# Slot order, channel-major share and recompute lead in a two-pass ConvNeXt-V2 block

## The chip, the cores and the metric

The kernel runs on one core of a Trainium2 chip. The metric is the device time of one execution in microseconds, given as the median of five runs. PE is the matrix engine, ACT the engine of activations, DVE the vector engine, POOL the general engine (GpSimd), SP the engine that here only issues DMAs.

## The reference

The input is one image of 512 x 512 pixels with 96 channels in bf16. E is 4 x 96 = 384.

```python
for i in range(K):
    for j in range(K):
        out = out + xp[:, i:i+H, j:j+W, :] * dw[i, j][None, None, None, :]
h = _layernorm(out, axis=-1)
h = jnp.einsum('bhwc,ce->bhwe', h, w1)
h = _gelu(h)
gx = jnp.sqrt((h * h).sum(axis=(1, 2), keepdims=True) + 1e-6)
nx = gx / (gx.mean(axis=-1, keepdims=True) + 1e-6)
h = grn_gamma * (h * nx) + grn_beta + h
h = jnp.einsum('bhwe,ec->bhwc', h, w2)
return x + h
```

A depthwise 3 x 3 convolution, LayerNorm over the channels, an expansion to 384 channels with GELU, a global response normalisation (GRN), a contraction to 96 channels and a residual. GRN needs, for each of the 384 channels, the sum of squares over all pixels of the image, so nothing of the contraction can start before the whole image has been expanded once.

## The kernel before

The image is cut into 128 blocks of four rows (2048 pixels). A block's pixels are handled as four quarters ("quads") of 512 columns. There are two passes.

**First pass.** A loop over slots s (lines 721 to 834); every engine executes its instructions in the order in which the program issues them (`InOrder`, line 22). In the steady state slot s does these things for different blocks:

- It convolves block s on PE in three bursts of 24 small matmuls (`conv_taps`, line 408), which all write one PSUM tile Y; the pool of Y has one buffer. After bursts 0 and 1 PE is drained (`pe.drain`, line 441). ACT copies Y to the SBUF tile `y_bf` (`evac`, line 443). Burst 0 of block s also reads rows of block s+1.
- DVE turns x of block s+2 to channels on partitions (`turn_x`, line 387).
- PE sums y and y squared over the channels for an earlier block (`stage_stats`, line 462, 24 matmuls of 4 columns) into the columns S of the PSUM tile SG; POOL makes the square `ysq`. After each batch of four blocks DVE reads the sums and clears S (`stage_moments`, line 474, a scaling and a memset), POOL works out the reciprocal deviation, DVE turns it (`stage_turn`, line 549), SP spreads it by DMA, and POOL multiplies (`stage_norm`, line 581).
- It expands one normalised block b, about 14 slots behind the convolution (`mlp_units`, line 611). The 2048 x 384 results are made in six expansions, each of two PSUM banks (pool `psU`, two buffers of two banks) and one GELU on ACT: `pair(0..2)` make quarters 0 and 1 with channels on the partitions ("channel-major"), 128 channels at a time, into `gsh`; `rest(0..2)` make the other two quarters into `gm`. A third quarter may be channel-major too (`cm_quads`, line 91): then the first half of `gm` is channel-major and the second half pixel-major. The pixel-major part has pixels on the partitions and 384 columns for each of four groups of 128 pixels in a quarter.
- It adds up squares for GRN in two ways. Channel-major quarters: DVE's bn_stats (`squares`, `squares_rest`), three for each quarter, entries collected 32 at a time and then aggregated by DVE (`combine`, line 671, three bn_aggr). Pixel-major quarters: PE multiplies each 128 x 128 piece by itself into a Gram accumulator whose diagonal is the sum (`gram_mms`, line 664), 12 matmuls a quarter, into the remaining columns of the tile SG. S (128 columns) and the Gram columns (384) fill one PSUM bank together. The Gram work of block b is done in the slot after its own.
- SP stores quarter 0 of `gsh` in HBM (`g_dram`).

The pools of `gsh` and `gm` have three buffers each. Blocks 126 and 127 are kept in SBUF (`is_res`) and are treated apart. From slot 128 on there is no convolution left, and the slots only expand.

**Second pass.** A loop over the blocks (line 898), kept ones first. For each block the contraction runs in four sub-steps of 48 / 4 = 12 matmuls into O (`stage_mm2`, line 282); DVE adds O to `xb` and SP writes the result. POOL loads x again and adds a bias to it (`stage_xb`, line 274). Quarter 0 comes back from HBM; quarters 1 to 3 are expanded again from the stored normalised input: three units a block, each of three matmuls of 512 columns and one GELU of 1536 columns (`recompute_units`, line 254). There are 384 units. After each sub-step `pace` (line 330) issues as many units as its formula asks for; they run ahead of the contraction by a lead that begins at LEAD = 8 units (line 316). `advance` never goes further than five blocks ahead.

The order in a slot that both convolves and expands (lines 782 to 815), as PE sees it: conv(0), pair(0), pair(1), conv(1), pair(2), conv(2), rest(0), statistics, rest(1), Gram of the block before, rest(2). ACT: pair 0, 1, 2, the copy of Y, rest 0, 1, 2.

Of the kernel before, what the change touches and what calls it, by code (L numbers as in the profile page):

```python
# [53 lines left out]
def kernel(  # L54
# [17 lines left out]
    E = w1.shape[1]  # L72
# [5 lines left out]
    NBLK = H // GR  # L78
# [9 lines left out]
    def is_res(q):  # L88
        return q >= NBLK - RES

    def cm_quads(q):
        return 3 if q % 3 and not is_res(q) else 2

    def kept_quads(q):
        return 2 if is_res(q) else 1
# [64 lines left out]
    with ExitStack() as p1:  # L160
# [74 lines left out]
        NSUB = PXP // GPS  # L235
# [82 lines left out]
        total = len(todo)  # L318
# [10 lines left out]

        def pace(n, sub):  # L330
            due = sum(1 for v in todo if v <= n + 1) if sub == NSUB - 1 else 0
            even = LEAD + (n * NSUB + sub + 1) * (total + 2 - LEAD) / (NSUB * NBLK)
            advance(max(due, even), n + PRE)

        SG = psS.tile([128, 2 * NS + NCH * 128], f32, name="SG")
# [72 lines left out]
        def conv_taps(b, spare):  # L408
            if spare:
                Ua = psU.tile([128, 2, W], f32, name="U")  # L410
                Ub = psU.tile([128, 2, W], f32, name="U")
                Y = [Ua[:, 0, :], Ua[:, 1, :], Ub[:, 0, :]]
            else:
                Y3 = psY.tile([128, NI, W], f32, name="Y")
                Y = [Y3[:, i, :] for i in range(NI)]
            mms = []
            for n in range(3):
                mms.append([(h, j, (n + h) % NI, dx) for dx in (0, -1, 1) for j in range(GR) for h in range(2)])
            flat = [m for ms in mms for m in ms]
            first = {}  # L420
            last = {}
            for n, (h, j, i, dx) in enumerate(flat):
                first.setdefault((i, j), n)
                last[i, j] = n

            def burst(n):
                k = sum(len(ms) for ms in mms[:n])
                for h, j, i, dx in mms[n]:
                    src = b + shift(h, j)
                    o0, o1 = max(0, -dx), W - max(0, dx)  # L430
                    pe.matmul(
                        Y[i][32 * j:32 * j + 32, o0:o1],
                        lhsT=Wq[64 * h:64 * h + 64, i, dx + 1, j, :],
                        rhs=x_rows(src, 64 * h, 64 * h + 64, i, MB * (1 + dx) + o0, o1 - o0)
                        if 0 <= src < NBLK else zrow[64 * h:64 * h + 64, o0:o1],
                        start=first[i, j] == k,
                        stop=last[i, j] == k,
                    )
                    k += 1
                if n < 2:  # L440
                    pe.drain()

            def evac():
                y = ypool.tile([128, NI, W], bf16, name="y_bf")
                if spare:
                    act.activation(out=y[:, 0:2, :], in_=Ua[:], func=ACTF.Identity)
                    act.activation(out=y[:, 2, :], in_=Ub[:, 0, :], func=ACTF.Identity)
                else:
                    act.activation(out=y[:], in_=Y3[:], func=ACTF.Identity)
                ybf[b] = y  # L450

            return [lambda n=n: burst(n) for n in range(3)], evac

        def stage_sq(b, on_act):
            q = ysqpool.tile([128, NI, W], bf16, name="ysq")
# [152 lines left out]
        def px0(b):  # L608
            return NCH * QW * (cm_quads(b) - 2)
# [51 lines left out]

            return pair, rest, squares, squares_rest, store

        def gram_mms(b):
            for k in range((TAIL - px0(b)) // E):
                for j in range(NCH):
                    c = px0(b) + k * E + j * 128
                    v = gms[b][:, c:c + 128]
                    pe.matmul(gram[:, j, :], lhsT=v, rhs=v, start=False, stop=True, skip_group_check=True)
# [51 lines left out]
        for s in range(last_slot + 1):  # L721
            get = lambda kind: at.get((s, kind), [])
            if s + 4 < NBLK:
                load_x(s + 4)
            for b in get("read"):
                stage_read(b)
            for b in get("write"):
                stage_write(b)
            for k in get("bcast"):
                stage_bcast(k)  # L730
            for k in get("rows"):
                stage_rows(k)
            if store:
                store()
                store = None
            for k in get("moments"):
                stage_moments(k)
            for k in get("newton"):
                stage_newton(k, pool)
            for b in get("norm"):  # L740
                stage_norm(b)
            for b in get("sqp"):
                stage_sq(b, False)
            for k in get("rstd"):
                stage_rstd(k, pool)
            mlp = get("mlp")

            def spread_out():
                for k in get("spread"):
                    stage_spread(k)  # L750
                for b in get("norma"):
                    stage_norm(b)

            spare = not mlp and s % 2 == 1
            taps, evac = conv_taps(s, spare) if s < NBLK else ([], None)
            if not mlp:
                for f in taps:
                    f()
                if not spare:
                    spread_out()  # L760
                if evac:
                    evac()
                for b in get("sqa"):
                    stage_sq(b, True)
                if s + 2 < NBLK:
                    turn_x(s + 2)
                for b in get("stats"):
                    stage_stats(b)
                if spare:
                    spread_out()  # L770
                for k in get("chain"):
                    stage_moments(k)
                    stage_chain(k)
                for k in get("turn"):
                    stage_turn(k)
                for b in get("gram"):
                    gram_mms(b)
            else:
                b = mlp[0]
                pair, rest, squares, squares_rest, put_out = mlp_units(b)  # L780
                conv = lambda n: taps[n]() if taps else None
                conv(0)
                pair(0)
                pair(1)
                if not taps:
                    for b2 in get("gram"):
                        if b2 != b:
                            gram_mms(b2)
                squares(0)
                conv(1)  # L790
                spread_out()
                if s + 2 < NBLK:
                    turn_x(s + 2)
                pair(2)
                squares(1)
                for k in get("turn"):
                    stage_turn(k)
                conv(2)
                if evac:
                    evac()  # L800
                rest(0)
                squares(2)
                for b2 in get("stats"):
                    stage_stats(b2)
                rest(1)
                if taps:
                    for b2 in get("gram"):
                        if b2 != b:
                            gram_mms(b2)
                rest(2)  # L810
                squares_rest()
                for b2 in get("gram"):
                    if b2 == b:
                        gram_mms(b2)
                if not is_res(b):
                    store = put_out
            if s == 1:
                setup_mlp()
            if s == 4:
                setup_rest()  # L820
            for b in get("combine"):
                combine(b)
            if s == last_slot - 3:
                pc.close()
                late.psO = p2.enter_context(tc.tile_pool(name="psO", side="right", bufs=2, space=bass.MemoryType.PSUM))
                late.xr = p2.enter_context(tc.tile_pool(name="xr", side="right", bufs=5))
                late.xb = p2.enter_context(tc.tile_pool(name="xb", side="right", bufs=3))
                late.gr = p2.enter_context(tc.tile_pool(name="gr", side="right", bufs=4))
                late.gl = p2.enter_context(tc.tile_pool(name="gld", side="right", bufs=6))
                late.o = p2.enter_context(tc.tile_pool(name="o", side="right", bufs=4))  # L830
            for n in {2: (0, 1, 2), 1: (3, 4)}.get(last_slot - s, ()):
                stage_load(n, sp, pool)
            if s == last_slot - 1:
                for n in range(RES):
                    stage_xb(ORDER[n], pool, B2bc_f)
# [104 lines left out]
```

## Time and profile before

| | |
|---|---|
| median of five runs | 1566.23 us (1563.24 to 1571.81) |
| profiled execution, its own time | 1563.24 us |
| profiled execution, span from first to last instruction | 1561.5 us |
| granted PE clock, mean | 0.996 |
| busy: PE, ACT | 1449.5 us, 1447.2 us (93% each) |
| busy: POOL, DVE | 1315.7 us (84%), 1129.5 us (72%) |
| bn_stats on channel-major quarters | 1020 instructions, 468.7 + 156.5 + 7.3 us |
| Gram matmuls | 2064, 136.3 us |
| slots with convolution and expansion | about 104 to 937 us |
| slots with expansion alone | 937 to about 1018 us |
| second pass | about 1020 to 1561 us |

The profile shows one execution on the chip. Times in it are microseconds from the first instruction. "Busy" of an engine is the time in which at least one of its instructions runs; instructions of one engine overlap a little at their ends, so the durations of single instructions add up to more than the time that a run of them takes. A line of a timeline gives the start, the time, the engine, the line of the code (L32 is the helper that issues all ordered instructions), the operation with its tiles, and in brackets how long the engine was idle before and what ended the wait.

### The profile page before, as it was taken

How to read it: one execution, taken by the hardware profiler on the slowest of the kernel's cores; microseconds unless marked ns; L12 is line 12 of the kernel's file. 1: busy time of each engine (PE TensorE's matmuls, PEld its weight loads, DVE VectorE, ACT ScalarE, POOL GpSimd, SP SyncE). 2: the span in 40 equal slices, each digit the busy share in tenths (PEclk: the TensorE clock that was granted, in tenths of full speed). 3: DMA queues.
4: the chain of work that ended last, by engine and by line, in shares of the span. 5: the costliest groups of instructions: out<-in, count | busy, mean ns of one | idle time of the engine just before them, and what ended most of it. 6: DMA issues, size and time to landing. Idle time of an engine off the chain costs nothing. (4 is left out here: it accounts for less than half of the span.)

```text
span 1561.5 us, 55720 instructions
## 1 busy us (share of the span) xinstructions
PE 1449.5 (93%) x23749; PEld 843.8 (54%) x23749; DVE 1129.5 (72%) x2027; ACT 1447.2 (93%) x1306; POOL 1315.7 (84%) x933
## 2 busy tenths in 40 slices
PE   7889999999999999999999997789999999999997
PEld 3444444444444444444444444457777777777765
DVE  6748978888898888889888888855555555555544
ACT  3889989999999999999999999999999999999996
POOL 3559888988989898998889887559999999999994
PEclk8999999999999999999999999999999999999999
DMA  5668787787778788777778667879999999999994
GB/s 147 183 186 262 233 253 221 241 256 213 238 237 250 214 249 253 221 236 239 230 225 249 209 189 221 280 252 391 388 390 391 385 395 385 384 379 390 383 369 147
DMA packets 235470, 427.94 MB, mean 274 GB/s; under 512 B 34102, under 2 KB 148374, under 8 KB 235222
## 3 DMA queue, kind: packets, MB, share of 16 engines
q1 hardware_dynamic: 219972, 356.59, 70.1%
q0 software_dynamic: 13888, 67.64, 11.4%
q8 instruction: 186, 3.05, 0.8%
q14 instruction: 62, 0.51, 0.1%
q10 hardware_dynamic: 1362, 0.15, 0.1%
HBM read 272.78 MB, written 150.72 MB: 271 GB/s over the span
## 5 line engine op out<-in xcount | busy, mean ns | idle before, releaser
L32 PE MATMUL U<-ynT,w1p 128*128 128x512 bf16 x2166 | 601.7, 380 | 44.1 <-ACT gm L32 8.4
L32 DVE BATCH_NORM_STATS2 bst<-gsh 128x6 f32<-128x512 bf16 x756 | 468.7, 673 | 128.3 <-ACT gsh L32 127.7
L32 ACT ACTIVATE gr<-U 128x1536 bf16<-128x1536 f32 (+1 forms) x384 | 521.1, 1450 | 16.3 <-PE U L32 14.2
L32 POOL TENSOR_TENSOR yn<-y_bf,rbc 128x1536 bf16<-128x1536 bf16 x128 | 397.2, 3106 | 83.5 <-ACT rbc L32 30.3
L32 DVE TENSOR_TENSOR o_sb<-O,xb 128x384 bf16<-128x384 f32 x512 | 277.6, 557 | 252.5 <-PE O L32 175.7
L278 POOL TENSOR_TENSOR xb<-xr,B2c 128x1536 f32<-128x1536 bf16 x126 | 395.1, 3137 | 38.0 <-DVE B2c L32 29.9
L32 ACT ACTIVATE gsh<-U 128x1024 bf16<-128x1024 f32 x378 | 369.5, 1024 | 55.3 <-ACT gm L32 29.2
L32 ACT ACTIVATE gm<-U 128x1024 bf16<-128x1024 f32 x384 | 367.9, 1033 | 0.1
L32 PE MATMUL Y<-xT,Wq 64*32 64x511 bf16 (+1 forms) x8694 | 321.4, 389 | 8.5 <-DVE B2bc_f L32 3.7
L32 POOL TENSOR_TENSOR ysq<-y_bf 128x1536 bf16<-128x1536 bf16 x114 | 313.4, 2750 | 13.8 <-ACT y_bf L32 13.5
L32 PEld LDWEIGHTS <-w1p 128*128 128x128 bf16 x2166 | 169.1, 97 | 277.6 <-issue 177.8
L32 PEld LDWEIGHTS <-gr 128*128 128x128 bf16 x4584 | 228.7, 98 | 84.9 <-ACT gr L32 12.1
L32 PE MATMUL O<-W2s,gr 128*128 128x96 bf16 x4584 | 251.4, 206 | 12.4 <-ACT gr L32 9.4
L32 PEld LDWEIGHTS <-Wq 64*32 64x32 bf16 x9216 | 101.9, 90 | 186.5 <-issue 145.8
L32 PE MATMUL U<-w1p,ynT 128*128 128x384 bf16 (+2 forms) x1032 | 161.3, 272 | 33.6 <-ACT gm L32 30.5
L32 ACT ACTIVATE y_bf<-Y 128x1536 bf16<-128x1536 f32 x121 | 175.1, 1447 | 16.6 <-PE Y L32 16.4
L32 DVE STREAM_TRANSPOSE xT<-xin 128x576 f32<-128x576 f32 (+1 forms) x256 | 181.3, 747 | 2.9 <-DMA xin<-in_x_dram 2.8
L32 DVE BATCH_NORM_STATS2 bst<-gm 128x6 f32<-128x512 bf16 x252 | 156.5, 677 | 0.9 <-ACT gm L32 0.9
L32 PEld LDWEIGHTS <-ynT 128*128 128x128 bf16 x1032 | 88.6, 97 | 90.8 <-issue 69.3
L32 PE MATMUL SG<-gm 128*128 128x128 bf16 x2064 | 136.3, 219 | 0.5 <-ACT gm L32 0.3
L32 PEld LDWEIGHTS <-gm 128*128 128x128 bf16 x2064 | 121.0, 98 | 11.5 <-issue 0.5
L250 POOL DMA_DIRECT2D xr<-in_x_dram x123 | 67.9, 552 | 27.6 <-POOL xb L278 27.6
(103 smaller groups left out, 700.7 us busy)
## 6 DMA issues: line engine op xcount, KB each, us to landing
ynT<-yn_dram SPq DMA_DIRECT2D x254, 384.0 KB
xin<-in_x_dram SPq DMA_DIRECT2D x126, 432.0 KB
yn_dram<-yn SPq DMA_DIRECT2D x512, 96.0 KB
xr<-in_x_dram POOLq DMA_DIRECT2D x128, 384.0 KB, 6.6
out_dram<-o_sb SPq DMA_DIRECT2D x127, 384.0 KB
g_dram<-gsh SPq DMA_DIRECT2D x126, 384.0 KB
gl<-g_dram SPq DMA_DIRECT2D x84, 384.0 KB
gl<-g_dram POOLq DMA_DIRECT2D x42, 384.0 KB, 6.7
```

The costliest lines, as they stand in the source:

```text
L32: r = f(*a, **k)
L250: pq.dma_start(out=xr[:], in_=x[0, r0:r0 + GR].rearrange("r w c -> (r w) c").rearrange("(p g) c -> p g c", g=PXP))
L278: pq.tensor_tensor(out=xb[:], in0=grp[q]["xr"][:], in1=bias[:, None, :].to_broadcast([128, PXP, C]), op=ALU.add)
```

## The change

Three things are changed.

1. Every block that is not kept in SBUF now has three channel-major quarters. Before, blocks whose number is divisible by three had two.
2. The order inside a slot that expands is another one. PE's new order is conv(0), pair(0), conv(1), pair(1), first half of the Gram matmuls of the block before, pair(2), second half, rest(0), conv(2), rest(1), statistics, rest(2). ACT's is pair 0, 1, 2, rest(0), the copy of Y, rest(1), rest(2). On DVE the transposes of x come ahead of the squares of pair(0), and the turn of the reciprocal deviation comes after the squares of pair(2). Where there is no convolution, the Gram matmuls stay together ahead of pair(2).
3. In the second pass the pace formula no longer lets the lead shrink from 8 units to 2: it stays at 8 until the units run out.

The bursts of the convolution also take an argument that can leave out the drain; no caller in the program sets it, so the drains stay.

```diff
     def cm_quads(q):
-        return 3 if q % 3 and not is_res(q) else 2
+        return 2 if is_res(q) else 3
...
         def pace(n, sub):
             due = sum(1 for v in todo if v <= n + 1) if sub == NSUB - 1 else 0
-            even = LEAD + (n * NSUB + sub + 1) * (total + 2 - LEAD) / (NSUB * NBLK)
+            even = LEAD + (n * NSUB + sub + 1) * total / (NSUB * NBLK)
             advance(max(due, even), n + PRE)
...
-            def burst(n):
+            def burst(n, fence=True):
...
-                if n < 2:
+                if n < 2 and fence:
                     pe.drain()
...
-        def gram_mms(b):
-            for k in range((TAIL - px0(b)) // E):
+        def gram_mms(b, part=None):
+            n = (TAIL - px0(b)) // E
+            for k in range(n) if part is None else range(n // 2) if part == 0 else range(n // 2, n):
...
                 pair, rest, squares, squares_rest, put_out = mlp_units(b)
-                conv = lambda n: taps[n]() if taps else None
+                conv = lambda n, fence=True: taps[n](fence) if taps else None
+
+                def gram_of_last(part):
+                    for b2 in get("gram"):
+                        if b2 != b:
+                            gram_mms(b2, part)
+
                 conv(0)
                 pair(0)
-                pair(1)
-                if not taps:
-                    for b2 in get("gram"):
-                        if b2 != b:
-                            gram_mms(b2)
-                squares(0)
                 conv(1)
                 spread_out()
                 if s + 2 < NBLK:
                     turn_x(s + 2)
+                pair(1)
+                squares(0)
+                if not taps:
+                    gram_of_last(0)
+                    gram_of_last(1)
+                if taps:
+                    gram_of_last(0)
                 pair(2)
                 squares(1)
+                if taps:
+                    gram_of_last(1)
+                rest(0)
+                squares(2)
                 for k in get("turn"):
                     stage_turn(k)
                 conv(2)
                 if evac:
                     evac()
-                rest(0)
-                squares(2)
+                rest(1)
                 for b2 in get("stats"):
                     stage_stats(b2)
-                rest(1)
-                if taps:
-                    for b2 in get("gram"):
-                        if b2 != b:
-                            gram_mms(b2)
                 rest(2)
                 squares_rest()
```

More of the change, by code (lines that the diff above doesn't have):

```diff
@@ L450, in evac @@
                 ybf[b] = y
-            return [lambda n=n: burst(n) for n in range(3)], evac
+            return [lambda fence=True, n=n: burst(n, fence) for n in range(3)], evac
         def stage_sq(b, on_act):
```

## The prediction

> **What bounds the kernel now.** I read the page first, then busy time by stretches, then the timelines of single engines. The stretches split the span into three regimes; columns are the stretch, its length, then busy us (with instructions) of PE, PEld, DVE, ACT, POOL, the clock, DMA share and GB/s.
>
> ```profile
> 400.00:600.00 200.00, 188.03 (x3410) 94.33 (x3406) 172.06 (x293) 187.38 (x187) 177.64 (x138) 1.00 0.78 239
> ...
> 935.00:1020.00 85.00, 62.90 (x536) 36.76 (x535) 72.51 (x123) 80.38 (x87) 51.61 (x36) 1.00 0.80 253
> 1200.00:1400.00 200.00, 197.80 (x2797) 143.97 (x2796) 105.60 (x197) 197.53 (x146) 187.76 (x116) 1.00 1.03 387
> ...
> 1500.00:1561.00 61.00, 49.69 (x677) 35.28 (x675) 26.77 (x49) 47.28 (x35) 39.88 (x21) 0.99 0.63 230
> ```
>
> From about 100 to 937 us a slot convolves one block and expands another: ACT is busy 187.4 of 200 us, PE 188.0, DVE 172.1. To 1013 us follow slots without a convolution. From 1030 us the second pass runs: ACT 197.5 of 200, PE 197.8, and only the last stretch is thin (ACT 47.3 of 61). With three engines above 93%, shares decide nothing; I need the wait that ends last inside a slot: two stretches of the timelines of PE and ACT (start, us, instructions, idle before and its releaser).
>
> ```profile
> 565.55 1.50 PE L32 MATMUL SG<-gm 128*128 128x128 bf16 x24
> ...
> 573.19 0.83 PE L32 MATMUL SG<-gm 128*128 128x128 bf16 x12
> 574.35 0.60 PE L32 MATMUL U<-w1p,ynT 128*128 128x256 bf16 x4 [0.33 <-ACT gm L32]
> 574.88 0.87 PE L32 MATMUL Y<-xT,Wq 64*32 64x512 bf16 x24
> 575.87 1.03 PE L32 MATMUL U<-ynT,w1p 128*128 128x512 bf16 x4
> ```
>
> ```profile
> 571.94 1.45 ACT L32 ACTIVATE y_bf<-Y 128x1536 bf16<-128x1536 f32 x1
> 573.28 2.85 ACT L32 ACTIVATE gm<-U 128x1024 bf16<-128x1024 f32 x3
> 576.56 2.93 ACT L32 ACTIVATE gsh<-U 128x1024 bf16<-128x1024 f32 x3 [0.43 <-ACT gm L32]
> ```
>
> Each slot ACT runs seven evacuations back to back and then idles 0.43 us (0.55 in some slots). The chain behind that gap: the sixth expansion, rest(2), needs the PSUM pair that ACT frees with rest(0). ACT starts rest(0) at 573.28, PE rest(2) at 574.35 (+1.07), the first convolution burst conv(0) at 574.88 (+0.53), pair(0) at 575.87 (+0.99, with its drain), ACT the result at 576.56 (+0.69): 3.28 us. ACT's own three evacuations cover 2.73. Slots of the three kinds of block take 7.44, 7.64 and 7.46 us (22.54 for three: ACT's first evacuation at 591.65, then 614.20, is the same). The 7.64 is the slot after a two-quarter block: 24 Gram matmuls (565.55, 1.50 us) in place of 12 (573.19, 0.83), and PE then doesn't wait at all.
>
> The second pass, ACT's timeline and one row of POOL's waits (total, times, longest):
>
> ```profile
> 1439.53 47.34 ACT L32 ACTIVATE gr<-U 128x1536 bf16<-128x1536 f32 x34
> 1487.09 4.24 ACT L32 ACTIVATE gr<-U 128x1536 bf16<-128x1536 f32 x3 [0.22 <-PE U L32]
> ...
> 1526.77 4.13 ACT L32 ACTIVATE gr<-U 128x1536 bf16<-128x1536 f32 x3 [0.51 <-PE U L32]
> ...
> 1552.20 4.13 ACT L32 ACTIVATE gr<-U 128x1536 bf16<-128x1536 f32 x3 [1.40 <-PE U L32]
> ```
>
> ```profile
> POOL xr L250 <- POOL xb L278: 27.0, 91, 0.3
> ```
>
> ACT runs its 1.36 us activations nearly gapless until 1487 us; then the gap per block grows, 0.22, 0.51, 1.40, always before an expansion that PE issued late: the recompute lead shrinks from 8 units to 2 (line 332). All ACT gaps from 1040 us on sum to 12.5 us: 2.8 before 1487, 9.8 after. POOL's waits list shows nearly only its own 0.3 us hand-over ahead of an x load, so POOL is full too: additions 123 apart run from 1028.91 to 1532.13, 4.09 us a block; ACT needs 3 x 1.3556 = 4.07 (151 activations in 204.7 us).
>
> **What the Trainium skill says.** "Perfetto Trace Analysis", Optimization Strategy: a consistent bubble on the saturated engine can mean too little PSUM for the next tile. The trace agrees: two U buffers, and the same 0.43 us each slot. "PSUM — Partial Sum Buffer", PSUM bank collisions: guard PSUM by bank and quadrant, not by address. Here the LayerNorm sums and the Gram accumulator share the tile SG, 512 columns, and the trace has Gram matmuls waiting for a memset of the other columns:
>
> ```profile
> 949.53 0.17 DVE L32 MEMSET SG<- 128x128 f32 x1
> 949.75 0.83 PE L32 MATMUL SG<-gm 128*128 128x128 bf16 x12 [0.22 <-DVE SG L32]
> ```
>
> "SBUF — State Buffer", Who interferes with whom: a DVE instruction with one SBUF input outside the two-port modes doesn't contend with GpSimd. The trace agrees for bn_stats: the square on POOL takes 2739 to 2772 ns whatever DVE does. So I add nothing to POOL.
>
> **The change part by part.**
>
> *Third channel-major quarter in all 126 stored blocks.* 42 blocks change. PE: 3 matmuls of 512 columns for four blocks of 384 (same columns), 12 Gram matmuls fewer: (1.50-0.83) = 0.67 us of PE in the next slot; the 7.64 slot becomes like the others. DVE: 3 more bn_stats. One is 673 ns long, but three in a row take 1.86 and six 3.66, a pitch of 0.593: +1.78 us. DVE per slot is then 9 x 0.593 + 1.34 (two transposes) = 6.68, plus 0.14 (moments, memset, turn: 0.56 a batch of four), plus 0.25 (an aggregation, 2.68 at 531.81, each 10.7 slots): 7.07 us. ACT and the second pass see the same sizes, as the kept quarter is the same one.
>
> *The new order inside a slot.* PE: conv(0), pair(0), conv(1), pair(1), half Gram, pair(2), half Gram, rest(0), conv(2), rest(1), statistics, rest(2); ACT: pair 0, 1, 2, rest(0), Y, rest(1), rest(2). The drains stay (fence is never passed as False). Time zero is ACT's start on Y. Y ends at 1.45 and is the only such buffer, so the next conv(0) starts at 1.50 (in the early slots a burst that waits for Y starts 0.05 after it, 104.04). Pair(0) 2.49; its buffer was freed at 2.41, so it doesn't wait. ACT takes it at 3.18, just as it ends rest(2) (1.34 + 2 x 0.91 = 3.16): the old bubble is gone. But conv(1) now stands between pair(0) and pair(1): conv(1) 3.02, pair(1) 4.01, ACT 4.70, where it was free at 4.12. The new bubble is 0.55 us. Then half Gram 4.45, pair(2) 4.77 (ready 5.46, ACT free 5.64), half Gram, rest(0) 5.76 (ready 6.45, ACT free 6.58), conv(2) to 7.07, ACT Y again at 6.58 + 0.91 = 7.49. Rest(1), the statistics (0.6) and rest(2) end on PE by 8.6, before conv(0) is allowed at 8.99. The loop is 7.50 us: 1.50 + 0.99 + 0.53 + 0.99 + 0.69 + 0.95 + 0.94 + 0.91. Against 7.513, over 110 slots with both: -1.5 us. The bubble moves; only the extra Gram goes.
>
> *What the move puts behind what.* The Gram half now follows pair(1), so it waits in PE's queue for that slot's moments and memset on DVE, and pair(2), all of PE and ACT stand behind it. DVE reaches the moments when it has the last bn_stats of rest(1): ACT's rest(1) ends at 2.37, so 3.05, memset done 3.55, Gram due 4.45: fine, 0.9 to spare, plus 0.17 on ACT. Behind an aggregation it is 2.68 later, and DVE regains 0.82 a slot. Before, an aggregation came each 12 blocks, a multiple of the batch of 4, moments right behind it (534.49), and the statistics waited 0.3. Now it comes each 10.7 blocks: of ten, three meet moments at once (6.23 against 4.45, less 0.17: 1.6 us), three a slot later (0.8), four not: 7 us. The trace of before has no such wait; bounds: 0, if the stalled slots let DVE catch up ahead, and 10 x 2.68 = 27, if DVE regains nothing and each aggregation is paid in full. I take +7. The transposes of x go ahead of the squares, done by about 4.4 against 8.99, when conv needs them: free, with 4 us of cover; DVE used to wait for ACT there. The turn of rstd goes behind squares(2); SP's row DMAs wait for it in its queue, but Y has moved as far: nothing. POOL's square for LayerNorm needs Y, which ends 0.9 later in the slot; its result is read two slots on, 6 us of cover. Statistics later: DVE's moments come over 2 us after them. No DMA is added.
>
> *Slots without a convolution.* 12 slots from 936.96 to 1006.83, 5.82 each; those behind 24 Gram matmuls take 6.2, others 5.56, ACT-bound. Now DVE has 9 x 0.593 + 0.25 = 5.59; I take 5.65: -2 us. DVE's lag at the end has the 2.5 us hole ahead of the last block to go into, and the 3.9 us wait of the scale chain behind PE's queue.
>
> *Recompute with full lead.* The target grows by 0.75 a sub-step instead of 0.738. With ACT gapless from 1030.04, 376 activations of 1.3556 end at 1539.7 instead of 1556.3. Then the lead is paid back: the last expansion is issued two activations before, at 1537.1, with 11 sub-steps of O left, paced by DVE's addition at 0.535: 5.9 us, and 2.6 from the last addition to the span's end: 1547, so -14.6. Lower bound: only the 9.8 us goes and the longer tail costs 1.9: -8. POOL could end the last addition by 1541.4 and is then 1.5 us ahead of its reader: it caps the gain close to there. I take -13.
>
> Sum: -1.5 + 7 - 2 - 13 = -9.5. The profiled execution took 1563.2 (span 1561.5 and 1.7 around it), so 1553.7; the median of the runs is 3.0 above it, so the forecast for a median is about 1556.
>
> **Rivals.** *A: both bubbles go* (8%). If ACT finds conv(1) done in time, DVE's 7.07 or ACT's 6.89 sets the slot, 7.15 with losses: -0.36 x 110 = -40 in place of -1.5 + 7, so 1566 - 55 = 1511. For: the summed idle of ACT is 0.42 a slot. Against: two buffers, a burst with its drain between two expansions, 3.28 us against 2.8 of cover.
>
> *B: the second pass gives little* (15%). POOL at 4.09 a block is slower than ACT at 4.07, and the chain of waits runs through its additions from 1153 to 1415; if it holds the second pass, the gain falls to some 4 us, and the sum is 0: 1566.
>
> *C: slower, DVE takes over the slot* (22%). Place: the Gram half behind the moments. At a pitch of 0.64 rather than 0.593 DVE needs 9 x 0.64 + 1.34 + 0.39 = 7.49 a slot, regains nothing of an aggregation, and PE pays the 27 us in place of 7; at 0.645 the slot grows by another 0.04, +4: 1556 + 20 + 4 = 1580. The sum turns positive at 16.5 us of Gram waits, a pitch of about 0.615. For: DVE at 94% of the slot, with a wait of PE and ACT hung on it. Against: the runs of 3, 4 and 6 show 0.59 to 0.60.
>
> **How the numbers follow.** The forecast has 55%, own range 1548 to 1566: slots +-0.04 us (4.4), Gram waits 0 to 15, second pass -8 to -14.6. For 8 in 10 I reach into B and C and leave out A: 1542 to 1576. No change means within 0.3%, 4.7 us, about what a measurement can tell. Faster: 0.55 x 0.93 + 0.08 + a little of B = 0.60; same 0.16; slower 0.24.
>
> **What would show it.** Three slots take 22.5 us with ACT's gap now ahead of its second activation, 0.5 to 0.6 long, none at the slot's start; conv(0) waits for Y about 0.4 us; Gram matmuls wait for DVE's memset of SG in some six slots, by 0.8 to 1.7; DVE at 94 to 95% of the slots; in the last 60 us ACT's gaps of 0.5 and 1.4 are gone and its last activation ends near 1540 less what the first pass changed. Wrong: a gap on ACT in more than one place a slot, PE waiting for SG in most batches, or a last stretch led by POOL's additions.

## The result, and the profile after

The changed kernel takes 1561.8 us (median of 30 runs, 1557.28 to 1565.16) against 1566.41 (51 runs of the kernel before on the same chips): a ratio of 0.9966, 95% interval 0.9958 to 0.9973, so 4.6 us less. The forecast was 1556. The profiled execution took 1562.12 us (span 1560.3), only 1.1 less than that of before: the profiled execution of before lies 3.2 us below its median, the one of after 0.3 above. The traces can therefore show where time moved, but the total is read from the runs.

Busy time by stretches of the kernel after; columns as in the prediction: stretch, length, then PE, PEld, DVE, ACT, POOL, clock, DMA share, GB/s.

```profile
323.00:328.00 5.00, 4.71 (x53) 2.44 (x53) 4.92 (x9) 2.50 (x3) 4.04 (x13) 0.66 0.65 184
400.00:600.00 200.00, 185.82 (x3294) 89.81 (x3301) 191.53 (x323) 186.05 (x188) 177.92 (x137) 1.00 0.78 240
1022.00:1030.00 8.00, 6.30 (x37) 3.90 (x37) 1.99 (x10) 4.58 (x4) 3.11 (x1) 0.57 0.17 51
1200.00:1400.00 200.00, 191.20 (x2683) 137.50 (x2682) 100.75 (x190) 193.10 (x142) 182.36 (x111) 1.00 1.02 371
1500.00:1560.00 60.00, 54.62 (x804) 40.47 (x802) 32.17 (x60) 49.85 (x37) 50.82 (x27) 0.99 0.79 290
```

In the slots (400 to 600) DVE has gone from 172.1 to 191.5 busy us of 200; the 126 added bn_stats (378 on `gm` in place of 252) are the cause. ACT and PE are a little less busy, which is where to look for stalls. In the second pass (1200 to 1400) ACT has fallen from 197.5 to 193.1 and PE from 197.8 to 191.2: something holds both more than before. The last stretch is fuller (ACT 49.9 of 60).

**The slot.** PE in a slot without a stall, and in one with (start, us, operation, idle before and its releaser):

```profile
564.37 0.49 PE L32 MATMUL SG<-gm 128*128 128x128 bf16 x6 [1.62 <-DVE SG L32]
...
576.05 0.87 PE L32 MATMUL Y<-xT,Wq 64*32 64x512 bf16 x24 [0.19 <-ACT y_bf L32]
577.03 0.60 PE L32 MATMUL U<-ynT,w1p 128*128 128x512 bf16 x2
577.57 0.89 PE L32 MATMUL Y<-xT,Wq 64*32 64x512 bf16 x24
578.56 0.60 PE L32 MATMUL U<-ynT,w1p 128*128 128x512 bf16 x2
579.00 0.50 PE L32 MATMUL SG<-gm 128*128 128x128 bf16 x6
...
583.45 0.87 PE L32 MATMUL Y<-xT,Wq 64*32 64x512 bf16 x24 [0.20 <-ACT y_bf L32]
```

Conv(0) to conv(0) is 583.45 - 576.05 = 7.40 us, and all undisturbed slots are alike; before, the mean of three was 7.51. Conv(0) starts 0.2 us after ACT has freed Y, pair(0) 0.98 later, conv(1) 0.54, pair(1) 0.99. ACT in the same stretch:

```profile
565.33 1.02 ACT L32 ACTIVATE gsh<-U 128x1024 bf16<-128x1024 f32 x1 [1.53 <-PE U L32]
...
574.53 1.47 ACT L32 ACTIVATE y_bf<-Y 128x1536 bf16<-128x1536 f32 x1
...
579.20 1.94 ACT L32 ACTIVATE gsh<-U 128x1024 bf16<-128x1024 f32 x2 [0.44 <-PE U L32]
```

From the copy of Y to ACT's second pair evacuation is 579.20 - 574.53 = 4.67 us, of which ACT idles 0.44. Before, the gap of 0.43 stood one evacuation earlier, at the first pair. The bubble has moved, as forecast. At 565.33 it is 1.53 us, because PE's Gram half waited 1.62 us at 564.37. What it waited for is on DVE:

```profile
561.14 2.77 DVE L32 BATCH_NORM_AGGREGATE mv<-bst 128x2 f32<-128x192 f32 x3
563.82 0.23 DVE L32 TENSOR_SCALAR mom<-SG 128x128 f32<-128x128 f32 x1
564.15 0.17 DVE L32 MEMSET SG<- 128x128 f32 x1
```

An aggregation of 2.77 us stands right ahead of the moments and the memset that Gram waits for. Between 110 and 935 us there are six such waits, 7.3 us together, the longest 1.6; the slot takes 9.05 us when moments stand directly behind an aggregation, 8.1 to 8.3 when they come one slot later. One slot took 10.51: its stall was followed by a lowered clock, 0.66 on average over the 5 us of the first row above. An early slot took 9.83, with PE waiting 2.5 us for POOL's `ysq`. The faster loop is worth 110 x 0.11 = 12 us, the stalls gave about 11 back: the last copy of Y starts at 933.27, one evacuation of 0.91 later in its slot than before, where it started at 932.92. The first pass through the convolution is thus some 0.6 us ahead.

**Slots without a convolution.** Twelve take 5.63 us each (936.40 to 1003.93) in place of 5.82. The second pass's first GELU starts at 1017.05 in place of 1020.24, 3.2 us ahead. ACT at the start of the second pass, after and then before:

```profile
1017.05 5.61 ACT L32 ACTIVATE gr<-U 128x1024 bf16<-128x1024 f32 x6 [1.20 <-PE U L32]
1023.87 2.79 ACT L32 ACTIVATE gr<-U 128x1536 bf16<-128x1536 f32 x2 [1.22 <-issue]
1028.86 1.45 ACT L32 ACTIVATE gr<-U 128x1536 bf16<-128x1536 f32 x1 [2.20 <-PE U L32]
```

```profile
1020.24 5.60 ACT L32 ACTIVATE gr<-U 128x1024 bf16<-128x1024 f32 x6 [1.20 <-PE U L32]
1026.79 2.79 ACT L32 ACTIVATE gr<-U 128x1536 bf16<-128x1536 f32 x2 [0.94 <-ACT gr L32]
1030.04 70.51 ACT L32 ACTIVATE gr<-U 128x1536 bf16<-128x1536 f32 x52 [0.46 <-PE U L32]
```

At the ninth activation only 1.2 us of the 3.2 are left (1028.86 against 1030.04), and 0.6 at the sixteenth (1038.79 against 1039.42). In this stretch PE's granted clock is low, 0.57 in 1022 to 1030 (1.00 before). e1_pace and e7_agg_late have the same second pass at the full clock. From the first of these activations to the sixteenth it is 19.2 us in both, and in the kernel before; in the kernel after it is 21.7.

**Second pass.** ACT, and POOL's waits from 1040 us (total, times, longest):

```profile
1195.21 12.35 ACT L32 ACTIVATE gr<-U 128x1536 bf16<-128x1536 f32 x9 [0.22 <-PE U L32]
1207.78 12.33 ACT L32 ACTIVATE gr<-U 128x1536 bf16<-128x1536 f32 x9 [0.22 <-PE U L32]
...
1347.03 1.45 ACT L32 ACTIVATE gr<-U 128x1536 bf16<-128x1536 f32 x1 [2.57 <-PE U L32]
...
1537.07 13.54 ACT L32 ACTIVATE gr<-U 128x1536 bf16<-128x1536 f32 x10 [0.22 <-PE U L32]
```

```profile
POOL xr L250 <- POOL xb L278: 35.0, 118, 0.3
POOL gl L245 <- PE O L32: 2.5, 1, 2.5
```

The gaps of 0.51 and 1.40 at the end are gone: the lead does what it says. But from 1195 us on ACT has a gap of 0.22 ahead of every ninth unit, and three blocks take 1207.78 - 1195.21 = 12.57 us, 4.19 a block, where before a block took 4.09. Whatever delays POOL delays ACT: POOL's one wait of 2.5 us for a buffer of stored quarters, at 1338.8, comes out as ACT's 2.57 at 1347. ACT's last activation ends at 1550.61 in place of 1556.33, 5.7 us earlier, and the tail behind it grew from 5.2 to 9.7 us, since the lead is paid back there: 1.2 us net in this execution.

Why POOL is slower can be read from its own timeline. After:

```profile
1204.99 3.13 POOL L278 TENSOR_TENSOR xb<-xr,B2c 128x1536 f32<-128x1536 bf16 x1
1208.42 0.56 POOL L250 DMA_DIRECT2D xr<-in_x_dram  x1 [0.30 <-POOL xb L278]
1209.00 3.13 POOL L278 TENSOR_TENSOR xb<-xr,B2c 128x1536 f32<-128x1536 bf16 x1
1212.42 0.56 POOL L250 DMA_DIRECT2D xr<-in_x_dram  x1 [0.30 <-POOL xb L278]
1212.98 0.54 POOL L245 DMA_DIRECT2D gl<-g_dram  x1
1213.53 3.13 POOL L278 TENSOR_TENSOR xb<-xr,B2c 128x1536 f32<-128x1536 bf16 x1
```

And before:

```profile
1197.79 3.14 POOL L278 TENSOR_TENSOR xb<-xr,B2c 128x1536 f32<-128x1536 bf16 x1
1200.86 0.56 POOL L245 DMA_DIRECT2D gl<-g_dram  x1
1201.41 0.54 POOL L250 DMA_DIRECT2D xr<-in_x_dram  x1
1201.97 3.14 POOL L278 TENSOR_TENSOR xb<-xr,B2c 128x1536 f32<-128x1536 bf16 x1
1205.40 0.56 POOL L250 DMA_DIRECT2D xr<-in_x_dram  x1 [0.30 <-POOL xb L278]
```

An x load (`xr`) refills the buffer that the addition just ahead of it in POOL's queue has read, so it waits 0.30 us for POOL's own addition: 118 times after, 91 times before. Where the load of a stored quarter (`gl`, one for three blocks) stands ahead of the x load, the wait vanishes under it (1201.41). Before, it stood ahead in 29 of 43 pairs, after in 1 of 43. No line of the diff touches these loads: line 906 issues them through `nc.gpsimd` rather than through the wrapper that fixes the order, and the scheduler, which places such instructions itself, put them otherwise: e1_pace shows that the new pace formula alone is enough for it, while e2_slot and e3_quads, with the old formula, keep the order of before (29 of 43). From one addition to the next it is 4.01 us with an x load alone (1204.99 to 1209.00), 4.53 with the stored-quarter load behind (1209.00 to 1213.53), and 4.18 with it ahead (in before: 1197.79 to 1201.97). Three blocks take 2 x 4.01 + 4.18 = 12.20 us in the good order and 12.55 in the bad one, which is ACT's period above.

### The profile page after: what moved, and what is told of

It reads as the page before. It is cut to its first block, busy times and chain, and to the rows that moved or that the text cites. A ratio compares the mean times of both kernels' runs of the same rounds, so it can differ in the third digit from the quotient of the medians.

```text
span 1560.3 us, 54608 instructions
## 1 busy us (share of the span) xinstructions
PE 1436.0 (92%) x23119; PEld 819.3 (53%) x23119; DVE 1211.2 (78%) x2157; ACT 1437.7 (92%) x1306; POOL 1318.8 (85%) x933
## 5 line engine op out<-in xcount | busy, mean ns | idle before, releaser
L32 PE MATMUL U<-ynT,w1p 128*128 128x512 bf16 x2292 | 665.1, 381 | 48.8 <-ACT gm L32 9.1
L32 ACT ACTIVATE gr<-U 128x1536 bf16<-128x1536 f32 (+1 forms) x384 | 519.9, 1455 | 14.9 <-PE U L32 12.6
L32 ACT ACTIVATE gm<-U 128x1024 bf16<-128x1024 f32 x384 | 381.9, 1047 | 2.4 <-PE U L32 2.2
L32 PEld LDWEIGHTS <-w1p 128*128 128x128 bf16 x2292 | 181.4, 98 | 288.9 <-issue 203.7
L32 PEld LDWEIGHTS <-gr 128*128 128x128 bf16 x4584 | 236.2, 98 | 109.3 <-issue 25.1
L32 DVE BATCH_NORM_STATS2 bst<-gm 128x6 f32<-128x512 bf16 x378 | 242.6, 679 | 30.3 <-ACT gm L32 30.3
L32 PEld LDWEIGHTS <-Wq 64*32 64x32 bf16 x9216 | 113.5, 90 | 209.4 <-issue 170.5
L32 PEld LDWEIGHTS <-gm 128*128 128x128 bf16 x1560 | 107.3, 98 | 66.5 <-issue 12.2
L32 PE MATMUL SG<-gm 128*128 128x128 bf16 x1560 | 126.7, 220 | 8.8 <-DVE SG L32 8.0
L32 PE MATMUL U<-w1p,ynT 128*128 128x384 bf16 (+2 forms) x780 | 126.5, 272 | 5.0 <-ACT gm L32 3.8
L32 PEld LDWEIGHTS <-ynT 128*128 128x128 bf16 x780 | 67.3, 97 | 35.3 <-issue 15.4
```

Source lines behind the costliest of these rows:

```text
L32: r = f(*a, **k)
```

## Experiments

Theories: **P**, POOL's queue holds the second pass, and the order of its loads decides the rate; **L**, the longer lead is worth what was forecast and something else lost it; **M**, DMA traffic is the limit of the second pass; for the slots, **S**, the Gram waits behind aggregations eat the faster loop.

**e1_pace: the lead alone, in the kernel before.**

```diff
-            even = LEAD + (n * NSUB + sub + 1) * (total + 2 - LEAD) / (NSUB * NBLK)
+            even = LEAD + (n * NSUB + sub + 1) * total / (NSUB * NBLK)
```

> Only the pace formula of the change, on the kernel before. Theory P (POOL's queue): with the full lead the loads of x and of the stored quarter stand the other way round in POOL's queue (42 of 42 stored-quarter loads behind the x load, 14 of 43 before), the x load waits 0.3 us for POOL's own addition each time, POOL needs 12.56 us for three blocks instead of about 12.27, and the second pass gains about 2 us: ratio 0.998 to 1.001, ACT gaps of 0.22 us before every ninth activation. Rival L (the forecast's step: the lead alone sets the end): -13 us, ratio about 0.992.

Measured: 1565.16 us against 1567.13, ratio 0.9992 (0.9979 to 1.0006). POOL's order turned into that of after (1 of 43 pairs), with ACT's gap of 0.22 ahead of each ninth unit:

```profile
1195.29 12.34 ACT L32 ACTIVATE gr<-U 128x1536 bf16<-128x1536 f32 x9 [0.22 <-PE U L32]
```

P holds, L falls: the lead alone is worth about 2 us (the interval allows -3.3 to +0.9), far from 13.

**e2_slot: the new slot order alone**, with two-quarter blocks and the old pace (the hunks of the diff from `burst` to `rest(2)`, without the other two).

> Only the new order inside the slot, with the old two or three quarters and the old pace. Theory S (shared SG bank): the loop is 7.40 us for all slots instead of 7.51, -12 us, but every aggregation now stands directly ahead of moments, each of some nine holds the Gram half by about 1.6 us, +15: sum -2 to +6 us, ratio 0.999 to 1.004, and PE waits for SG about nine times. Rival: the waits come only from DVE's higher load (third quarter in all blocks); then no such waits here and -10 to -12 us, ratio 0.993.

Measured: 1584.16 us, 1.0109 (1.0088 to 1.0129): 17 us slower, a miss. PE's waits from 110 to 955 us:

```profile
PE SG L32 <- DVE SG L32: 13.0, 8, 1.6
```

With 32 entries to an aggregation and 2 2/3 quarters a block on average, an aggregation comes every 12 blocks, three batches of four exactly, so all eight meet moments right behind them, 1.6 us each: that is S at its worst. And the loop gains nothing: slots of 7.37, 7.40 and, behind 24 Gram matmuls, 7.84 have a mean of 7.54. That makes 13 + 110 x 0.03 = 16 us. Eight waits and their size were foreseen; that the mean slot would gain nothing was not.

**e3_quads: the third channel-major quarter alone.**

```diff
-        return 3 if q % 3 and not is_res(q) else 2
+        return 2 if is_res(q) else 3
```

> Only the third channel-major quarter in all blocks, old slot order, old pace. By the working in the prediction: the 7.64 us slot becomes 7.45, -7 us over 110 slots, and -2 us in the slots without a convolution; no Gram matmul waits for DVE, since the Gram work is last in the slot: -8 us, ratio 0.994 to 0.996. Rival D (DVE's load itself costs): slots above 7.5 us, ratio 1.000 or more.

Measured: 1558.27 us, 0.9948 (0.9930 to 0.9967), 8.9 less, nearly twice what the whole change brings. All slots take 7.45. This part is right by itself.

**e4_glfirst: the kernel after, with the loads of the second pass in program order.**

```diff
-                stage_load(n + PRE, nc.sync, nc.gpsimd)
+                stage_load(n + PRE, nc.sync, pool)
```

> The changed kernel with POOL's loads kept in program order, so that the load of the stored quarter always stands ahead of the x load. Theory P: the 0.3 us wait is hidden behind that issue, POOL needs 4.01 + 4.01 + 4.18 = 12.2 us for three blocks instead of 12.56, ACT's 4.07 a block sets the pace, and 9 to 11 us come off the changed kernel: about 1551 us, ratio to before 0.990. Rival M (the DMA engines, at a share of 1.02 to 1.03 in the second pass, hold it): the traffic is the same, so no change against the changed kernel, ratio 0.9965.

Measured: 1546.09 us, 0.9861 (0.9838 to 0.9883), 15.7 less than after; more than expected. POOL's timeline, its waits from 1040 us, and ACT in the second pass:

```profile
1202.56 0.56 POOL L32 DMA_DIRECT2D xr<-in_x_dram  x1
1203.38 3.12 POOL L278 TENSOR_TENSOR xb<-xr,B2c 128x1536 f32<-128x1536 bf16 x1 [0.26 <-DVE o_sb L32]
1206.45 0.55 POOL L32 DMA_DIRECT2D xr<-in_x_dram  x1
1207.41 3.12 POOL L278 TENSOR_TENSOR xb<-xr,B2c 128x1536 f32<-128x1536 bf16 x1 [0.40 <-DVE o_sb L32]
```

```profile
POOL xb L278 <- DVE o_sb L32: 28.9, 83, 1.0
```

```profile
1038.65 497.16 ACT L32 ACTIVATE gr<-U 128x1536 bf16<-128x1536 f32 x370
```

The expected mechanism was that the stored-quarter load would stand ahead and hide one wait in three. It does stand ahead now, in 42 of 43 pairs, but there is more: every load is issued one addition later in POOL's queue than it was, so its buffer has long been read, and no x load waits at all. POOL waits for its reader DVE instead, so it is no longer the limit, and ACT runs 370 activations in 497.16 us, 1.344 each, with no gap shown. The same loads cross the same queues, which excludes M.

**e5_order_before: the same edit of the loads in the kernel before**, with the shrinking lead.

> The kernel before with POOL's loads kept in program order, the old shrinking lead. Theory P: each x load then refills a buffer whose addition lies one addition further back, so its 0.3 us wait goes and POOL drops out as a bound; but ACT's gaps of 0.22, 0.51 and 1.40 us at the end (9.8 us) come from the shrinking lead and stay: only the 2.8 us of gaps before 1487 us and some small ones go, -2 to -5 us, ratio 0.997 to 0.999. Rival: POOL's queue alone held the second pass, and -12 us come without the lead, ratio 0.992.

Measured: 1563.23 us, 0.9983 (0.9971 to 0.9994), 3 less. No x load waits for an addition any more, and ACT then stands in the gaps that the lead of 2 leaves:

```profile
1513.90 4.13 ACT L32 ACTIVATE gr<-U 128x1536 bf16<-128x1536 f32 x3 [0.51 <-PE U L32]
...
1543.08 4.13 ACT L32 ACTIVATE gr<-U 128x1536 bf16<-128x1536 f32 x3 [1.40 <-PE U L32]
```

The lead alone gives 2 and the order alone 3, but on top of the lead the order gives 15.7 (e4_glfirst against after): two limits at nearly the same level, each of which hides the other.

**e7_agg_late: the kernel after, with an aggregation one slot later, behind that slot's moments.**

```diff
                 stage_moments(k)
+            for b in at.get((s - 1, "combine"), []):
+                combine(b)
...
-            for b in get("combine"):
-                combine(b)
+            if s == last_slot:
+                for b in get("combine"):
+                    combine(b)
```

> The changed kernel with one edit in the first pass: DVE aggregates the bn_stats of a block one slot later, behind the moments of that slot instead of ahead of them. Theory S: no Gram half meets a late memset any more, so the six waits of PE for SG (7.3 us), and the slow PE clock behind one of them (1.4 us), go: -7 to -9 us against the changed kernel, ratio to before 0.991 to 0.992. Rival D: DVE's load itself is the cost, and the waits only move to squares or transposes: 0 to -2 us, ratio 0.995 to 0.997.

Measured: 1555.96 us, 0.9928 (0.9910 to 0.9946), 5.8 less than after, short of the 7 to 9 expected, though the interval reaches them. No slot of 9.05 is left, three of 8.1 to 8.3 are:

```profile
PE SG L32 <- DVE SG L32: 3.4, 6, 0.9
```

These six waits (110 to 955 us) take 3.4 us in place of the 8.0 that seven take there in after. Two of the six, 0.9 us each, are at moments one slot after an aggregation: DVE still hasn't regained its 2.7 us by then.

**e8_both: e4_glfirst and e7_agg_late together.**

> The changed kernel with both edits: POOL's loads in program order and the later aggregation. They act in different passes, so the gains should add: e4_glfirst (1546 us) less 7 to 9 us, 1537 to 1539 us, ratio 0.981 to 0.982. Rival: something common (the start of the second pass, PE's clock) takes part of it back, ratio 0.984 or more.

Measured: 1539.99 us, 0.9829 (0.9809 to 0.9850). 1546.09 - 5.8 = 1540.3: the two add up, they lie in different passes.

**e9_old_slot: the kernel before with the third quarter, the full lead and the order of loads, but its own slot order** (the diffs of e3_quads, e1_pace and e4_glfirst).

> The old slot order with the other two parts of the change (third quarter in all blocks, full lead) and POOL's loads in program order. By the sums so far: e3_quads (1558 us), -2 for the lead alone and -15.7 for the order of the loads: 1541 us, ratio 0.983. If the new slot order is worth having at all, e8_both must be below it by 0.05 us in each of 110 slots, 5 us.

Measured: 1543.36 us, 0.9852 (0.9830 to 0.9873). Against e3_quads the lead and the order of the loads together give 14.9. The second pass can also be taken by itself, from ACT's first GELU in it to the end of the span; this leaves out the first pass, which differs between executions by several us:

| lead, order of the loads | first GELU | span | second pass |
|---|---|---|---|
| shrinking, the scheduler's, 29 of 43 `gl` ahead (before) | 1020.24 | 1561.5 | 541.3 us |
| full, the scheduler's, 1 of 43 ahead (e1_pace) | 1019.65 | 1560.3 | 540.7 us |
| shrinking, the program's (e5_order_before) | 1021.17 | 1557.9 | 536.7 us |
| full, the program's (e4_glfirst) | 1020.81 | 1544.6 | 523.8 us |
| full, the program's (e9_old_slot) | 1019.16 | 1542.9 | 523.7 us |

The lead is worth 0.6 us with the scheduler's order and 12.9 with the program's; the order 4.6 without the full lead and 16.9 with it; both 17.5.

For the slots: against e4_glfirst (1546.09) the new slot order with its Gram waits costs 2.7 us; with the aggregation put off (e8_both) it gains 3.4; these two differences are within the intervals. 110 slots x (7.45 - 7.40) = 5.5 us is what the shorter loop by itself has to offer here.

**e10_gram_early: e8_both with the first Gram half ahead of conv(1).**

```diff
                 pair(0)
+                if taps:
+                    gram_of_last(0)
                 conv(1)
...
-                if taps:
-                    gram_of_last(0)
                 pair(2)
```

> e8_both with one half of the Gram matmuls moved from behind pair(1) to behind pair(0), ahead of conv(1): the same work on every engine. Loop theory: copy of Y, conv(0), pair(0), conv(1), pair(1) and three evacuations follow each other, so 0.33 us of PE inside that chain lengthens a slot from 7.40 to 7.73 us in slots without moments, 110 x 0.33 = 36 us in all (more where moments hold the Gram half), ratio 1.005 or more. Rival (DVE or ACT load sets the slot, PE has slack): slots stay within 0.05 us of 7.40, ratio 0.983 to 0.987.

Measured: 1611.39 us, 1.0293 (1.0269 to 1.0318). PE:

```profile
570.19 0.87 PE L32 MATMUL Y<-xT,Wq 64*32 64x512 bf16 x24 [0.19 <-ACT y_bf L32]
...
571.61 0.70 PE L32 MATMUL SG<-gm 128*128 128x128 bf16 x6
572.25 0.86 PE L32 MATMUL Y<-xT,Wq 64*32 64x512 bf16 x24
573.23 1.03 PE L32 MATMUL U<-ynT,w1p 128*128 128x512 bf16 x4
...
578.12 0.88 PE L32 MATMUL Y<-xT,Wq 64*32 64x512 bf16 x24 [0.20 <-ACT y_bf L32]
```

The slot is 578.12 - 570.19 = 7.93 us, 0.53 more, so whatever stands between the copy of Y and pair(1) does lengthen the slot, though every engine has the same work as in e8_both: the loop, not the load, sets 7.40. The size was low: from the first of six Gram matmuls to the next group it is 572.25 - 571.61 = 0.64 us there and 0.33 in their old place (579.00 to 579.33 in the kernel after). Being due earlier, they also met the memset 25 times, for 17.0 us: 110 x 0.53 + 17.0, less the 3.1 of such waits that e8_both has, makes 72 us; measured are 71.4.

**e11_agg_spread: e8_both with the three bn_aggr of an aggregation in three successive slots.**

```diff
+        owed = []
...
-                    nr = min(32, NENT - 32 * k)
-                    for j in range(NCH):
-                        dve.bn_aggr(out=mv[:, j, k, :], in_=bst[:, j, :nr, :].rearrange("p a s -> p (a s)"))
+                    owed.extend((k, j, bst) for j in range(NCH))
+
+        def aggregate(n):
+            for k, j, bst in owed[:n]:
+                nr = min(32, NENT - 32 * k)
+                dve.bn_aggr(out=mv[:, j, k, :], in_=bst[:, j, :nr, :].rearrange("p a s -> p (a s)"))
+            del owed[:n]
...
             for b in at.get((s - 1, "combine"), []):
                 combine(b)
+            aggregate(1)
...
             if s == last_slot:
                 for b in get("combine"):
                     combine(b)
+                aggregate(len(owed))
```

> e8_both with the three bn_aggr of an aggregation in three successive slots, one each behind the moments. Theory S: DVE is then at most 0.9 us late at any moments, which the 0.9 + 0.17 us of slack cover: the four waits of PE for SG (3.1 us) go, no slot of 8.3 us is left, about 1537 us, ratio 0.981. Rival: DVE, at 95% of a slot, is late for other reasons and the waits stay.

Measured: 1535.58 us, 0.9805 (0.9785 to 0.9825), the fastest of all, 30.8 less than before. What is left of the waits:

```profile
PE SG L32 <- POOL ysq L32: 1.9, 1, 1.9
PE SG L32 <- DVE SG L32: 0.7, 1, 0.7
```

With 0.9 us at a time DVE keeps its place, and the new slot order with spread aggregations is 1543.36 - 1535.58 = 7.8 us below e9_old_slot (the intervals of the two ratios are just apart). That is more than the 5.5 of the loop. What the spreading would give in the old slot order wasn't tried, nor were sums and Gram columns put in separate banks, which would have tested the sharing of SG by itself.

## Why the prediction was right, and where it was off

- **The total.** Forecast -9.5 us, measured -4.6: the right direction at half the size. That the total fell within the range given was in part luck: the loop came out 11 us better than forecast and the lead 11 worse, and these two errors cancel.
- **The step that was off: "I take -13" for the full lead.** It measured 2 (e1_pace, in the medians) and 0.6 in the second pass by itself. The lead does have that worth, 12.9, where POOL is out of the way (e5_order_before against e4_glfirst). What failed is the step from there: "POOL could end the last addition by 1541.4 and is then 1.5 us ahead of its reader: it caps the gain close to there". It took POOL's 4.09 us a block, 0.02 from ACT's 4.07, as given. That figure was itself an average over an order of two loads that the scheduler chose, 29 pairs of one kind and 14 of the other; with 42 of the slower kind it became 4.19, and 0.1 us more in each of some 120 blocks is about the 12 us that are missing. The row of 0.3 us waits was on the page and was read as a constant cost, not as one that depends on what stands ahead. Rival B named POOL as the limit, at an unchanged 4.09, and put the gain at 4.
- **ACT's 4.07 was not its own rate either,** but the rate at which the shrinking lead fed it: at the start of the second pass 52 activations take 70.51 us before (1.356 each), and 53 take 71.30 in e1_pace, whose only edit is the lead (1.345 each, 4.03 a block). POOL's 4.09 was thus more than 0.02 away; it runs from the start of the first addition to the end of the 123rd, and from start to start it is 4.10. Part of the sum for the lead was also made wrongly: 1537.1 + 5.9 + 2.6 is 1545.6, not 1547.
- **"The loop is 7.50 us": right in kind, a little too long.** It measured 7.40. The terms stand in the prediction's order 1.52, 0.98, 0.54, 0.99, 0.64 and 2.73 (for 1.50, 0.99, 0.53, 0.99, 0.69 and 0.95 + 0.94 + 0.91 = 2.80): the excess was in the handover to ACT and in the last three evacuations. Over 110 slots that is another 11 us gained against the forecast. That it is a loop through the single Y buffer, and not a load, is shown by e10_gram_early. The moved bubble was forecast at 0.55 and is 0.44.
- **"I take +7" for the Gram waits: right** (7.3 in six waits, the longest 1.6 as worked out). The Trainium skill, "PSUM — Partial Sum Buffer", PSUM bank collisions, says to guard PSUM by bank and quadrant and not by address. The kernel is guarded so, as its trace shows: Gram matmuls wait for the memset of other columns of the same tile, and one meeting costs up to 1.6 us. Not foreseen: one early wait for `ysq` of 2.5 us (0.7 before, 4.3 in e3_quads, 1.9 in e11_agg_spread), and a lowered clock behind a stall.
- **The third quarter: right**, and larger alone than the forecast of -1.5 us for the loop suggests. With 7.45 us for every slot (e3_quads) it gains 7 us in the loop; a new loop of 7.50 means that the new order was expected to take most of that back. Measured, the new order gains another 0.05 a slot. Not said in the prediction: it is also what makes the new order bearable, since it moves aggregations out of step with the moments (e2_slot against after).
- **Slots without a convolution: right**, 5.65 forecast, 5.63 measured.
- **Rivals.** A (both bubbles go) didn't occur. C (DVE takes over) didn't either: six bn_stats in a row still take 3.6 us where they wait for nothing in between, a pitch of 0.59.
- **The remainder.** For the profiled execution the terms add up. First pass: loop -12, stalls +11, slots without a convolution -2.3, which makes -3.3 where the first GELU came 3.2 earlier. Second pass: -0.6 as in e1_pace, +2.6 in the stretch with the low clock: +2.0 (543.3 in place of 541.3). Together -1.3, and the span is 1.2 shorter. The medians differ by 4.6; the profiled execution of before is 3.2 faster than its median, and why wasn't settled.

## What to carry to other kernels

Instructions whose place a scheduler chooses are part of every change, even of one that doesn't name them: read their order in the built kernel before and after, and ask of each small repeated wait what stands ahead of it. When two engines stand within one or two per cent of each other, lifting one limit can give little and lifting both much more (here 0.6 and 4.6 us singly, 17.5 together), so test changes in pairs before one of them is thrown away. A periodic chore on a nearly full engine (here 2.7 us each 10.7 slots) is best cut into pieces and kept behind what others wait for; its period against that of its victim decides how often they meet.

## What the runs showed of the hardware

- **The clock after short stalls.** In the execution shown PE's granted clock is 0.50 from 323.4 to 326.8 us, behind a wait of 1.62 us, and 0.50 from 1023.1 to 1029.9, around one of 1.24. The profile of e11_agg_spread has 0.50 from 1012.4 to 1019.2, at the same place in the program; the other ten have the full clock there, before too, with the same wait of 1.24 us. Elsewhere in the program eight of those ten have such a stretch, of 3.4 or 6.8 us (from 60 us on, the last microseconds left out); before and e8_both have none. A wait of about 1.6 us is not enough to bring it: of three in after one was followed by it (323.3, and not 564.4 and 803.8), and of eight in e2_slot one. What decides it stays open.
- **Where a matmul stands changes its time.** From the first of six Gram matmuls of 128 columns to the next group of matmuls it is 0.33 us when an expansion follows and 0.64 when a burst of the convolution's 64 x 32 tiles does (e10_gram_early). The cause wasn't looked into.
- **A DMA issue on POOL that waits for POOL's own addition** pays 0.30 us after the addition has ended; with another issue of 0.54 us between them it pays nothing.
